# Low-weight products of features 128 to 191 on 64 rows of TensorE, two side by side into two PSUM banks

## The chip, the cores and the metric

The kernel runs on one core of one Trainium2 chip. The metric is the device time of one execution in microseconds (us); lower is better. A core has five engines with queues of their own: TensorE (PE, matrix products into PSUM; PEld is its weight load), VectorE (DVE), ScalarE (ACT), GpSimd (POOL) and SyncE (SP, which here only issues DMAs).

## What is computed

An attention-like step turns 8 x 3584 tokens of 192 features into 28672 rows, and a mixture of 8 experts with one expert for each token (top 1) follows.

```python
x_unf = x_pad[:, idx, :].reshape(B, S, K, H, group)          # K = 7 taps, H = 8 heads
out = np.einsum('bshk,bskhg->bshg', softmax(weight_gen), x_unf)
x = out.reshape(28672, 192)
e_idx = np.argmax(x @ w_gate, axis=1)
for e in range(8):
    h = np.maximum(x[mask] @ w1[e], 0.0)                     # 192 -> 1024
    ye = h @ w2[e]                                           # 1024 -> 192
    out[mask] = gate_w[mask, None] * eom[mask, e, None] * ye
```

## The kernel before

**Stages.** The tokens are worked through in 32 units of 896. For a unit, DVE and POOL multiply taps and weights and the sums are formed on PE or DVE; the rows are split into fp16 high and low parts, gated, and scattered by expert into a buffer in HBM (`srtd`). As soon as enough rows of an expert lie there, a *tile* of T rows (T = 256 or 384 in the first rounds, then 512, and at the end a mix of 512, 256 and 128) goes through the expert. There are 81 tiles. Until the last unit is scattered, tiles and attention run together; after that (the *late part*) only tiles are left.

**A tile.** `tile_load` (L944) issues on SP, in this order: `meta`, a transposing DMA of the rows into `xT`, and the expert's weights `wa` (L953, w1 in fp16 parts) and `wb` (w2). `xT` has three blocks of 128 partitions: block 0 is the high part of features 0 to 127, block 1 holds the high part of features 128 to 191 on partitions 0 to 63 and their low part on 64 to 127, block 2 is the low part of features 0 to 127.

**GEMM1** (`gemm1_unit`, L959). A *unit of GEMM1* fills one PSUM bank of 512 columns: nf = 512 // T blocks of 128 hidden features, five products each, all on 128 rows of the array:

```python
for q, (wo, k) in enumerate(((f * P, 0), (1024 + f * P, 0), (f * P, 2), (b3, 1), (b3 + 512, 1))):
    T_.matmul(ps[:, at + i * T : at + (i + 1) * T], lhsT=wa[:, wo : wo + P], rhs=xT[:, k, 0:T], start=(q == 0), stop=(q == 4), ...)
```

The fourth multiplies the high weights of features 128 to 191, which lie in `wa` twice (partitions 0 to 63 and 64 to 127), with block 1; the fifth multiplies their low weights, also stored twice, with block 1, so its lower half is low weight times low feature. `evac_steps` (L972) then empties the bank: ACT writes relu as fp16 (`hh`), DVE the rest (`hl`).

**GEMM2** (`gemm2_group`, L981) takes 128 rows of a tile: 24 products of 192 columns. `gemm_steps` (L1066) places two units of GEMM1, then a group of GEMM2, and so on. For T = 512 and 384 a tile has eight units (four twos), for 256 four, for 128 two.

**Order.** The program orders itself while it is built: each chain of steps yields the engine that it needs next, `Order.step` (L88) takes the chain that can start first by costs in the program (`tensor_cost`, L195, and others), and what comes out is the fixed order of each engine's queue. A change of a cost or of a step can so move any instruction.

**Weights.** `weight_steps` (L425) loads w1 and w2 of each expert, `split_steps` (L439) scales and splits them and stores them to HBM as `wd`, 3585 words of 4 bytes for each partition: 2048 for `wa`, 1537 for `wb`.

Of the kernel before, what the change touches and what calls it, by code (L numbers as in the profile page):

```python
# [9 lines left out]
F16 = mybir.dt.float16  # L10
BF16 = mybir.dt.bfloat16
F32 = mybir.dt.float32
I32 = mybir.dt.int32
# [3 lines left out]

P = 128
W = 194
WW = 3585  # L20
RMAX = 24
NE = 8
MASK = 0x3F800000
# [170 lines left out]

def tensor_cost(name, args, kwargs):  # L195
    o = kwargs.get("rhs", kwargs.get("in_"))
    return max(60, largest((o,), {}) + 6) * (4 if o.dtype == F32 else 1) / 2400.0


# [18 lines left out]
def kernel(ctx: ExitStack, tc: tile.TileContext, x, wg, wgate, wogate, w1, w2, cst, out):  # L218
    nc = tc.nc
    od = Order()  # L220
# [24 lines left out]
    late = []  # L245
# [89 lines left out]
    o = 256  # L335
# [89 lines left out]
    def weight_steps(stg):  # L425

        for e in range(NE):
            yield from take(st_free, SP)

            st1 = stg.tile([P, 1536], F32, tag="st1", name=f"st1_{e}")  # L430
            st2 = stg.tile([P, 1536], F32, tag="st2", name=f"st2_{e}")
            SP.dma_start(out=st1[:, 0:1024], in_=w1[e, 0:128, :])
            for h in range(2):
                SP.dma_start(out=st1[64 * h : 64 * h + 64, 1024:1536], in_=w1[e, 128:192, 512 * h : 512 * h + 512])
            SP.dma_start(out=st2.rearrange("p (c d) -> p c d", d=D), in_=w2[e].rearrange("(c p) d -> p c d", p=P))
            od.add(split_steps(e, st1, st2), (RANK_W, e), S)
            od.cur.t = od.now

    def split_steps(e, st1, st2):  # L439
        sqd = stg_sq.tile([P, 1536], BF16, tag="sqd", bufs=1, name=f"sqd{e}")  # L440
        ss = sp.tile([P, 2], F32, tag="wss", name=f"wss{e}")
        S.activation(sqd, st1, AF.Square, accum_out=ss[:, 0:1])
        yield S
        S.activation(sqd, st2, AF.Square, accum_out=ss[:, 1:2])
        yield from take(tr_free, T_)
        pg = ps[:, 1536:1538]
        T_.matmul(pg[:, 0:2], lhsT=ones32, rhs=ss, start=True, stop=True)
        yield V
        sc = sp.tile([P, 2], F32, tag="wsc", name=f"wsc{e}")
        inv = sp.tile([P, 2], F32, tag="winv", name=f"winv{e}")  # L450
        yield from scales(pg[:, 0:2], sc, inv, f"w{e}", tr_free)
        s1, s2 = sc[:, 0:1], sc[:, 1:2]
        yield from take(wa_free, S)
        wa = wp.tile([P, 1536], I32, tag="wa", bufs=WA, name=f"wpa{e}")
        wah = wa.bitcast(F16)

        for lo, n in ((0, 1024), (2048, 512)):
            src = st1[:, lo // 2 : lo // 2 + n]
            hi = wah[:, lo : lo + n]
            yield S  # L460
# [11 lines left out]
        wb = wp.tile([P, WW - 2048], I32, tag="wb", bufs=WB, name=f"wpb{e}")  # L472
# [9 lines left out]
        SP.dma_start(out=wd[e, :, 2048:WW], in_=wb)  # L482
        wb_free.append((od.cur.t, "wb"))
        state["weights"] += 1

# [458 lines left out]
    def tile_load(t, T, ti, i, writers, ka, kb):  # L944
# [6 lines left out]
        xT = gp.tile([P, 3, 512], F16, tag="xT", bufs=XB, name=f"xT{t}")  # L951
        loaded(SP.dma_start_transpose(out=xT[:, :, 0:T], in_=rows.bitcast(F16)[:, 0:384]), writers)
        wa = (late[0] if ka == "late" else wp).tile([P, 2048], I32, tag="wa", bufs=LATE_W if ka == "late" else WA, name=f"wa{t}")  # L953
        SP.dma_start(out=wa, in_=wd[bass.ds(e, 1), :, 0:2048].rearrange("a p c -> p (a c)"))
        wb = (late[0] if kb == "late" else wp).tile([P, WW - 2048], I32, tag="wb", bufs=LATE_W if kb == "late" else WB, name=f"wb{t}")
        SP.dma_start(out=wb, in_=wd[bass.ds(e, 1), :, 2048:WW].rearrange("a p c -> p (a c)"))
        return dict(t=t, T=T, G=Gn, units=8 // (512 // T), wa=wa.bitcast(F16), wb=wb.bitcast(F16), inv=wb.bitcast(F32)[:, 1536:1537], meta=meta, xT=xT, ka=ka, kb=kb, hh=[], hl=[], hl_t=0.0)

    def gemm1_unit(hp, d, u, at):  # L959

        t, T, wa, xT = d["t"], d["T"], d["wa"], d["xT"]
        nf = 512 // T
        hh = hp.tile([P, 512], F16, tag="hh", name=f"hh{t}_{u}")
        hl = hp.tile([P, 512], F16, tag="hl", name=f"hl{t}_{u}")
        for i in range(nf):
            f = u * nf + i
            b3 = 2048 + f // 4 * 1024 + f % 4 * P
            for q, (wo, k) in enumerate(((f * P, 0), (1024 + f * P, 0), (f * P, 2), (b3, 1), (b3 + 512, 1))):
                T_.matmul(ps[:, at + i * T : at + (i + 1) * T], lhsT=wa[:, wo : wo + P], rhs=xT[:, k, 0:T], start=(q == 0), stop=(q == 4), skip_group_check=True)
        od.add(evac_steps(d, ps[:, at : at + nf * T], hh[:, 0 : nf * T], hl[:, 0 : nf * T], at), (RANK_H,), S, T_.t + LAT_P)  # L970

    def evac_steps(d, src, hh, hl, at):  # L972
        S.activation(hh, src, AF.Relu)
# [7 lines left out]
    def gemm2_group(d, g, at):  # L981
# [4 lines left out]
        py = ps[:, at : at + D]  # L986
        nf = 512 // T
        for f in range(8):
            lo = (f % nf) * T + g * P
            hh = d["hh"][f // nf][:, lo : lo + P]  # L990
            hl = d["hl"][f // nf][:, lo : lo + P]
# [74 lines left out]
    def gemm_steps(hp):  # L1066
# [3 lines left out]
        while True:  # L1070
            moved = False
            if cur is None and ahead:
                cur, i = ahead.pop(0), 0
            if cur is not None and len(h_free) >= 2:
                for _ in range(2):
                    _, at = yield from take(hu_free, T_)
                    yield from take(h_free, T_)
                    od.cur.t = max(od.cur.t, cur["ready"])
                    gemm1_unit(hp, cur, i, at)
                    i += 1  # L1080
# [70 lines left out]
LAT_P = 0.3  # L1151
# [25 lines left out]
FIRST_G = ()  # L1177
DEFER = 6
WBX = 5.0
PAIRS = 0  # L1180
TURN_SP = True
GT = 1
# [22 lines left out]
```

## Time and profile before

| | |
|---|---|
| median of 3 runs | 1276.98 us (1276.81 to 1280.58) |
| the profiled execution | 1277.73 us, its span 1276.0 us |
| mean granted clock of TensorE | 0.977 |
| busy: PE, DVE, POOL, ACT | 1143.7, 997.5, 895.6, 602.5 us |
| moved by DMA | 300.24 MB |

The profile gives each engine's busy time, the idle time before a group of instructions and what ended it. A matmul's record begins when its columns start to enter and ends, by a model, when its result is out, so records of successive products overlap. A timeline row of n products lasts n - 1 pitches and one record; the pitch, start to start, is what a product costs in a full queue.

### The profile page before, as it was taken

To read this page: it belongs to the slowest core of one execution; us is meant where nothing else is said; L and a number is where in the kernel's file an instruction comes from. 1 tells how busy PE (TensorE), PEld (TensorE's weight loads), DVE (VectorE), ACT (ScalarE), POOL (GpSimd) and SP (SyncE) were. 2 spreads that over 40 slices of the span, in tenths; PEclk is the share of its full clock that TensorE was granted. 3 is DMA by queue.
4 is the path that set the end of the run, shared out by engine and by line. 5 is a ranking of instruction groups with operands and counts; after the bars stand their busy time and mean duration, and the time that the engine had idled before them with its cause. 6 is when DMAs were issued, how large, how long until landed. Compare 5 with 4: busy or idle time off the path is not lost.

```text
span 1276.0 us, 28173 instructions
## 1 busy us (share of the span) xinstructions
PE 1143.7 (90%) x9958; PEld 832.0 (65%) x9958; DVE 997.5 (78%) x2135; ACT 602.5 (47%) x1305; POOL 895.6 (70%) x773
## 2 busy tenths in 40 slices
PE   5788778888988898969999999999999999979998
PEld 2444347666655666646666666666667779868998
DVE  7899968888999898989999999989998633323332
ACT  3676444545544445534554545545455444433443
POOL 6769877878687689989688898798987544312222
PEclk9899988999999999989999999999999999999999
DMA  9887568888988677768886977876686789999993
GB/s 298 268 242 244 188 207 222 240 209 247 251 195 241 184 215 182 233 171 229 243 217 192 240 219 210 253 215 212 191 223 163 223 296 315 351 274 314 321 343 131
DMA packets 273054, 300.24 MB, mean 235 GB/s; under 512 B 211478, under 2 KB 232839, under 8 KB 262544
## 3 DMA queue, kind: packets, MB, share of 16 engines
q1 hardware_dynamic: 250928, 253.83, 69.0%
q0 software_dynamic: 21840, 44.30, 11.3%
q8 instruction: 78, 1.28, 0.4%
q14 instruction: 64, 0.52, 0.2%
q10 hardware_dynamic: 144, 0.31, 0.1%
HBM read 196.42 MB, written 62.01 MB: 203 GB/s over the span
## 4 chain that ended last, share of the span: by engine, by line
PE 38%; DVE 29%; DMA 11%; issue 9%; POOL 7%; SPq 4%; ACT 2%; POOLq 0%; DVEq 0%; ACTq 0%
PE ps L151 38%; DVE ps L151 12%; DVE hl L151 6%; SPq L125 4%; POOL gap L151 3%; DMA w<-in_wg_dram 2%; DMA wa<-wd 2%; DVE rt L151 2%; DVE vap L151 2%; DMA srtd<-rt,posi 2%; POOL srtd L151 2%; DMA wb<-wd 1%; POOL out_dram L151 1%; DVE cx L151 1%; DVE wpa L151 1%
## 5 line engine op out<-in xcount | busy, mean ns | idle before, releaser
L151 PE MATMUL ps<-xT,wa 128*128 128x512 f16 (+3 forms) x3240 | 556.5, 322 | 49.2 <-DMA wa<-wd 30.1
L151 PE MATMUL ps<-wb,hh 128*128 128x192 f16 x3696 | 479.3, 247 | 16.0 <-ACT ys L151 4.5
L151 PE MATMUL ps<-wb,hl 128*128 128x192 f16 x1848 | 456.2, 247 | 0.7 <-DVE hl L151 0.7
L151 DVE SCALAR_TENSOR_TENSOR hl<-ps,hh 128x512 f16<-128x512 f32 (+1 forms) x476 | 309.2, 665 | 182.2 <-ACT hh L151 181.8
L151 PEld LDWEIGHTS <-wa 128*128 128x128 f16 x3240 | 278.0, 99 | 238.9 <-issue 34.3
L151 POOL TENSOR_TENSOR gap<-x,w 128x960 f32<-128x960 f32 (+5 forms) x268 | 373.6, 1419 | 27.9 <-PE ps L151 15.3
L151 PEld LDWEIGHTS <-hh 128*128 128x128 f16 x3696 | 337.1, 98 | 63.7 <-issue 22.6
L151 ACT ACTIVATE hh<-ps 128x512 f16<-128x512 f32 (+1 forms) x476 | 274.4, 583 | 215.1 <-PE ps L151 211.5
L151 POOL DMA_INDIRECT out_dram<-ys,meta x216 | 214.2, 991 | 221.3 <-ACT ys L151 160.2
L151 POOL DMA_INDIRECT srtd<-rt,posi x224 | 231.3, 1033 | 92.1 <-issue 56.9
L151 ACT ACTIVATE ys<-ps,sc 128x192 f32<-128x192 f32 x231 | 97.1, 421 | 240.1 <-PE ps L151 152.0
L151 DVE TENSOR_TENSOR ps<-ps,gap 128x1344 f32<-128x1344 f32 x125 | 194.0, 1552 | 4.9 <-POOL gap L151 4.0
L151 PEld LDWEIGHTS <-hl 128*128 128x128 f16 x1848 | 181.6, 98 | 1.1 <-DVE hl L151 0.9
L151 PE MATMUL ps<-gap,cf 128*128 128x512 f32 x168 | 72.9, 574 | 0.2 <-POOL gap L151 0.2
L151 POOL TENSOR_TENSOR gap<-halo,w 128x1152 f32<-128x1152 f32 (+4 forms) x38 | 61.9, 1628 | 13.6 <-DVE w L151 7.4
L151 DVE SCALAR_TENSOR_TENSOR rt<-ps,sx,rt 128x448 f16<-128x448 f32 x64 | 57.8, 908 | 16.3 <-ACT rt L151 12.7
L151 PE MATMUL ps<-vap,cf 128*128 128x512 f32 (+1 forms) x126 | 57.8, 603 | 14.0 <-DVE vap L151 14.0
L151 PE MATMUL ps<-gm,gt 128*128 128x32 f16 x672 | 27.8, 177 | 36.3 <-ACT ys L151 10.0
L151 PEld LDWEIGHTS <-gt 128*128 128x128 f16 x672 | 25.1, 97 | 46.6 <-issue 38.4
L151 DVE TENSOR_TENSOR vap<-x,w 128x960 f32<-128x960 f32 (+4 forms) x31 | 54.7, 1789 | 0.0
L151 PEld LDWEIGHTS ps<-gap,cf 128*128 128x128 f32 x168 | 32.5, 203 | 31.6 <-issue 29.1
L151 ACT ACTIVATE rt<-ps 128x1344 bf16<-128x1344 f32 x32 | 41.3, 1291 | 18.5 <-DVE ps L151 9.5
(115 smaller groups left out, 813.8 us busy)
## 6 DMA issues: line engine op xcount, KB each, us to landing
wa<-wd SPq DMA_DIRECT2D x81, 1024.0 KB
wb<-wd SPq DMA_DIRECT2D x81, 768.5 KB
x<-in_x_dram SPq DMA_DIRECT2D x32, 672.0 KB
w<-in_wg_dram SPq DMA_DIRECT2D x32, 196.0 KB
wd<-wpb SPq DMA_DIRECT2D x8, 768.5 KB
st<-in_w_dram SPq DMA_DIRECT2D x8, 768.0 KB
st<-in_w_dram SPq DMA_DIRECT2D x8, 512.0 KB
wd<-wpa SPq DMA_DIRECT2D x8, 512.0 KB
```

The source lines that it names most:

```text
L125: r = f(*args, **kwargs)
L151: r = f(*args, **kwargs)
```

## The change

- GEMM1's fifth product, low weights of features 128 to 191, now takes 64 rows: low weights times the high part of the features alone (the product of low weight and low feature is no longer formed).
- `gemm1_pair` replaces `gemm1_unit`. It takes two banks and two units with blocks f = 2 f2 and 2 f2 + 1: four full products (of each block) into the first bank; then the 64-row products, for block 2 f2 on partitions 0 to 63 into the first bank and for block 2 f2 + 1 on partitions 64 to 127 into the second; then four full products into the second.
- For the lower 64 partitions `xT` gets a fourth block: `again_steps` copies, on ACT, once for each tile, the high part of features 128 to 191 from partitions 0 to 63 to partitions 64 to 127.
- The low weights are stored once: `wa` goes from 2048 to 1792 words for each partition (1024 to 896 KB for a tile), `wd` from 3585 to 3329. The stores of `wpa` become six for each expert instead of five, and two loads of w1 are read in pieces of 128 columns.
- The cost of a product with 64 rows becomes half of its columns and 0.05 us.

```diff
-WW = 3585
+WA_W = 1792
+WW = 3329
...
+    if o.shape[0] == 64:
+        return 0.5 * largest((o,), {}) / 2400.0 + SWITCH
...
-                SP.dma_start(out=st1[64 * h : 64 * h + 64, 1024:1536], in_=w1[e, 128:192, 512 * h : 512 * h + 512])
+                SP.dma_start(
+                    out=st1[64 * h : 64 * h + 64, 1024:1536].rearrange("p (c d) -> p c d", d=P),
+                    in_=w1[e, 128:192, :].rearrange("p (c two d) -> p two c d", two=2, d=P)[:, h])
...
-                SP.dma_start(out=wd[e, 64 * q : 64 * q + 64, 1024 + 512 * h : 1536 + 512 * h], in_=wa[64 * h : 64 * h + 64, 1024:1536])
+                SP.dma_start(out=wd[e, 64 * q : 64 * q + 64, 1024 + 256 * h : 1280 + 256 * h], in_=wa[64 * h : 64 * h + 64, 1024:1280])
+        SP.dma_start(out=wd[e, :, 1536:1792], in_=wa[:, 1280:1536])
...
+    def again_steps(d):
+        S.copy(d["xT"][64:128, 3, 0 : d["T"]], d["xT"][0:64, 1, 0 : d["T"]])
+        d["again"] = True
...
-    def gemm1_unit(hp, d, u, at):
+    def gemm1_pair(hp, d, u):
+        for v in range(2):
+            _, at = yield from take(hu_free, T_)
+            yield from take(h_free, T_)
+            if u + v == 0:
+                yield T_, lambda: "again" in d
...
+            if v == 1:
+                for i in range(nf):
+                    for s in range(2):
+                        lo, f2, to = 64 * s, u // 2 * nf + i, ats[s] + i * T
+                        T_.matmul(ps[:, to : to + T], lhsT=wa[lo : lo + 64, 3072 + f2 * P : 3072 + f2 * P + P], rhs=xT[lo : lo + 64, 1 + 2 * s, 0:T], start=(s == 1 and i == 0), stop=(s == 0), skip_group_check=True)
+                od.add(evac, (RANK_H,), S, T_.t + LAT_P)
+            for i in range(nf):
...
+                for q, (wo, k) in enumerate(((f * P, 0), (1024 + f * P, 0), (f * P, 2), (b3, 1))):
+                    T_.matmul(ps[:, at + i * T : at + (i + 1) * T], lhsT=wa[:, wo : wo + P], rhs=xT[:, k, 0:T], start=(v == 0 and q == 0 and i == 0), stop=(v == 1 and q == 3), skip_group_check=True)
+            evac = evac_steps(d, ps[:, at : at + nf * T], hh[:, 0 : nf * T], hl[:, 0 : nf * T], at)
+        od.add(evac, (RANK_H,), S, T_.t + LAT_P)
...
                 cur, i = ahead.pop(0), 0
+                od.add(again_steps(cur), (RANK_H,), S, max(od.now, cur["ready"]))
...
+SWITCH = 0.05
```

Where the order moves, two places. On SP, where the first tile is loaded (`x8` and `w8` are the inputs of attention unit 8, `wpb7` is the store of the last expert's w2, `meta0`, `xT0`, `wa0`, `wb0` are tile 0), the queue had before:

```order
L125 DMA w8_1158<-in_wg_dram 128x392
L125 DMA halo_83<-in_x_dram 112x1152
L125 DMA halo_83<-in_x_dram 15x1152
L125 DMA x8_1162<-in_x_dram 128x1344
L125 DMA wd_79<-wpb7_1120 128x1537
L125 TENSOR_LOAD ti2_0_1146
L125 ISA x2
L125 TENSOR_LOAD ti2_0_1146
L125 ISA x3
L125 DMA meta0_1331<-srtd_78 128x2x2
```

The inputs of unit 8 stood ahead of the last store of weights and of tile 0. In the changed kernel the same queue has:

```order
L126 ISA x3
L126 DMA meta0_1275<-srtd_78 128x2x2
L126 ISA
L126 DMA_TRANSPOSE xT0_1277<-srtd_78 128x3x256
L126 ISA
L126 DMA wa0_1279<-wd_79 128x1792
L126 ISA
L126 DMA wb0_1281<-wd_79 128x1537
L126 DMA w8_1327<-in_wg_dram 128x392
L126 DMA halo_83<-in_x_dram 112x1152
L126 DMA halo_83<-in_x_dram 15x1152
L126 DMA x8_1331<-in_x_dram 128x1344
```

Tile 0 now stands one attention unit earlier, ahead of the inputs of unit 8, and its `wa` is smaller. On ACT, in the middle of the program, where tile 21 or 22 is emptied (`hh22_4` is unit 4 of tile 22, `ys21` a group of GEMM2 of tile 21), the queue had before:

```order
L151 ACTIVATE hh22_4_7733<-ps_82 128x512
L151 ACTIVATE hh22_5_7746<-ps_82 128x512
L151 ACTIVATE ys21_7493<-ps_82,sc21_7494 128x192
L151 ACTIVATE hh22_6_7789<-ps_82 128x512
L151 ACTIVATE hh22_7_7800<-ps_82 128x512
L151 ACTIVATE hh23_0_7839<-ps_82 128x512
```

The two units of each two followed each other, with nothing of the next tile between. In the changed kernel, at tile 21:

```order
L152 ACTIVATE hh21_4_7409<-ps_82 128x512
L152 ACTIVATE hh21_5_7416<-ps_82 128x512
L152 ACTIVATE ys20_7308<-ps_82,sc20_7309 128x192
L152 ACTIVATE hh21_6_7461<-ps_82 128x512
L152 COPY xT22_7258<-xT22_7258 64x512
L152 ACTIVATE hh21_7_7472<-ps_82 128x512
```

The copy for the next tile, 22, stands between the last two bank emptyings of tile 21, and it waits for the landing of `xT22`.

## Rows read from the trace of the kernel before

**Rows 1.** The page, part 2: the span in 40 equal slices of 31.9 us, busy share of each engine in tenths, the granted clock and the DMA engines.

```profile
PE   5788778888988898969999999999999999979998
DVE  7899968888999898989999999989998633323332
POOL 6769877878687689989688898798987544312222
PEclk9899988999999999989999999999999999999999
DMA  9887568888988677768886977876686789999993
```

**Rows 2.** Busy time by stage; the columns are the stretch, its length, then PE, PEld, DVE, ACT and POOL with their instructions, the granted clock, the DMA share and GB/s.

```profile
0.00:200.00 200.00, 152.11 (x674) 83.01 (x675) 170.10 (x323) 106.89 (x185) 153.58 (x111) 0.93 0.75 234
200.00:400.00 200.00, 169.87 (x1516) 125.78 (x1514) 186.30 (x411) 95.78 (x234) 153.40 (x134) 0.97 0.86 232
400.00:1000.00 600.00, 557.54 (x4807) 393.26 (x4805) 546.91 (x1218) 292.28 (x661) 502.55 (x442) 0.99 0.76 213
1000.00:1100.00 100.00, 100.00 (x1009) 81.30 (x1007) 43.13 (x114) 41.63 (x87) 41.48 (x43) 1.00 0.93 298
1100.00:1150.00 50.00, 43.39 (x509) 38.18 (x507) 13.74 (x20) 16.32 (x34) 13.29 (x14) 0.97 0.96 304
1150.00:1276.00 126.00, 120.78 (x1454) 110.46 (x1452) 37.36 (x54) 49.57 (x107) 31.27 (x32) 1.00 0.88 275
```

**Rows 3.** The same stretches, of the instructions on the tile `wa` alone (GEMM1): the columns are PE and PEld, the clock, the DMA share and GB/s of the whole core.

```profile
0.00:200.00 200.00, 10.82 (x74) 8.63 (x75) 0.93 0.75 234
200.00:400.00 200.00, 96.01 (x479) 46.28 (x476) 0.97 0.86 232
400.00:1000.00 600.00, 305.46 (x1283) 121.56 (x1284) 0.99 0.76 213
1000.00:1100.00 100.00, 56.40 (x433) 33.83 (x431) 1.00 0.93 298
1100.00:1150.00 50.00, 24.16 (x269) 18.00 (x267) 0.97 0.96 304
1150.00:1276.00 126.00, 63.63 (x710) 49.64 (x708) 1.00 0.88 275
```

**Rows 4.** Groups of PE's instructions with their shapes: count, busy us, mean ns of one record, idle time before.

```profile
L151 PE MATMUL ps<-xT,wa 128*128 128x512 f16 x1680 | 400.6, 382 | 32.7 <-DMA wa<-wd 16.9 <-DVE hl L151 14.9
...
L151 PE MATMUL ps<-xT,wa 128*128 128x128 f16 x880 | 52.7, 219 | 3.1 <-DMA wa<-wd 3.1
L151 PE MATMUL ps<-xT,wa 128*128 128x384 f16 x280 | 51.9, 332 | 9.2 <-DMA wa<-wd 5.9 <-DVE hl L151 3.4
L151 PE MATMUL ps<-xT,wa 128*128 128x256 f16 x400 | 51.4, 289 | 4.2 <-DMA wa<-wd 4.2
```

**Rows 5.** Timeline of PE, one row of products for each size of tile: start, duration, count.

```profile
423.15 2.32 PE L151 MATMUL ps<-xT,wa 128*128 128x512 f16 x10
...
235.09 1.79 PE L151 MATMUL ps<-xT,wa 128*128 128x384 f16 x10
...
1224.98 2.35 PE L151 MATMUL ps<-xT,wa 128*128 128x256 f16 x20
...
1220.77 2.40 PE L151 MATMUL ps<-xT,wa 128*128 128x128 f16 x40
```

**Rows 6.** Timeline of PE where the form of the products changes: 32 columns after 192, with a weight load for each; then in attention from 32 columns to transposes to fp32.

```profile
427.21 0.25 PE L151 MATMUL ps<-wb,hl 128*128 128x192 f16 x1
427.29 0.46 PE L151 MATMUL ps<-gm,gt 128*128 128x32 f16 x12
...
169.97 0.30 PE L151 MATMUL ps<-gm,gt 128*128 128x32 f16 x6
170.12 0.33 PE L151 MATMUL ps<-ident,rt 128*128 128x128 f16 x3
170.29 2.47 PE L151 MATMUL ps<-vap,cf 128*128 128x512 f32 x6
```

**Rows 7.** PE's waits, longest in total first: us, times, longest.

```profile
PE ps L151 <- DMA wa<-wd: 30.1, 11, 9.6
PE ps L151 <- DVE hl L151: 19.0, 23, 3.8
PE ps L151 <- ACT ys L151: 17.1, 29, 2.2
```

**Rows 8.** SP's queue about the first tile's load (start, duration), and the DMA issues of the weights of a tile.

```profile
148.44 0.35 SPq L125 DMA_DIRECT2D w<-in_wg_dram  x1
...
164.11 0.41 SPq L125 DMA_DIRECT2D meta<-srtd  x1
...
170.64 0.34 SPq L125 DMA_DIRECT2D w<-in_wg_dram  x1
...
wa<-wd SPq DMA_DIRECT2D x81, 1024.0 KB
wb<-wd SPq DMA_DIRECT2D x81, 768.5 KB
```

**Rows 9.** ACT's copies of fp16 and its bank emptying, with shapes: count, busy us, mean ns.

```profile
L151 ACT ACTIVATE hh<-ps 128x512 f16<-128x512 f32 x420 | 247.1, 595 | 195.2 <-PE ps L151 191.9 <-issue 3.1
...
L151 ACT COPY gt<-ps 128x768 f16<-128x768 f16 x18 | 14.3, 794 | 18.5 <-PE ps L151 18.3
...
L151 ACT COPY gt<-ps 128x384 f16<-128x384 f16 x6 | 2.9, 479 | 4.2 <-PE ps L151 4.2
```

More of the change, by code (lines that the diff above doesn't have):

```diff
@@ L471, in split_steps @@
         yield from take(wb_free, S)
-        wb = wp.tile([P, WW - 2048], I32, tag="wb", bufs=WB, name=f"wpb{e}")
+        wb = wp.tile([P, WW - WA_W], I32, tag="wb", bufs=WB, name=f"wpb{e}")
         wbh = wb.bitcast(F16)
@@ L481, in split_steps @@
         yield SP
-        SP.dma_start(out=wd[e, :, 2048:WW], in_=wb)
+        SP.dma_start(out=wd[e, :, WA_W:WW], in_=wb)
         wb_free.append((od.cur.t, "wb"))
@@ L950, in tile_load @@
         loaded(SP.dma_start(out=meta[:, 0:Gn, :], in_=rows[:, W - 2 : W].rearrange("(g p) c -> p g c", p=P)), writers)
[L951 to L954, printed above, removed]
@@ L955, in tile_load @@
-        wb = (late[0] if kb == "late" else wp).tile([P, WW - 2048], I32, tag="wb", bufs=LATE_W if kb == "late" else WB, name=f"wb{t}")
-        SP.dma_start(out=wb, in_=wd[bass.ds(e, 1), :, 2048:WW].rearrange("a p c -> p (a c)"))
-        return dict(t=t, T=T, G=Gn, units=8 // (512 // T), wa=wa.bitcast(F16), wb=wb.bitcast(F16), inv=wb.bitcast(F32)[:, 1536:1537], meta=meta, xT=xT, ka=ka, kb=kb, hh=[], hl=[], hl_t=0.0)
-    def gemm1_unit(hp, d, u, at):
-        t, T, wa, xT = d["t"], d["T"], d["wa"], d["xT"]
[L962 to L970, printed above, removed]
+        xT = gp.tile([P, 4, 512], F16, tag="xT", bufs=XB, name=f"xT{t}")
@@ new lines, in tile_load @@
+        loaded(SP.dma_start_transpose(out=xT[:, 0:3, 0:T], in_=rows.bitcast(F16)[:, 0:384]), writers)
+        wa = (late[0] if ka == "late" else wp).tile([P, WA_W], I32, tag="wa", bufs=LATE_W if ka == "late" else WA, name=f"wa{t}")
+        SP.dma_start(out=wa, in_=wd[bass.ds(e, 1), :, 0:WA_W].rearrange("a p c -> p (a c)"))
+        wb = (late[0] if kb == "late" else wp).tile([P, WW - WA_W], I32, tag="wb", bufs=LATE_W if kb == "late" else WB, name=f"wb{t}")
+        SP.dma_start(out=wb, in_=wd[bass.ds(e, 1), :, WA_W:WW].rearrange("a p c -> p (a c)"))
@@ new lines, in tile_load @@
+        return dict(t=t, T=T, G=Gn, units=8 // (512 // T), wa=wa.bitcast(F16), wb=wb.bitcast(F16), inv=wb.bitcast(F32)[:, 1536:1537], meta=meta, xT=xT, ka=ka, kb=kb, hh=[], hl=[], hl_t=0.0)
+    def again_steps(d):
+        S.copy(d["xT"][64:128, 3, 0 : d["T"]], d["xT"][0:64, 1, 0 : d["T"]])
+        d["again"] = True
+        return
+        yield
+    def gemm1_pair(hp, d, u):
+        t, T, wa, xT = d["t"], d["T"], d["wa"], d["xT"]
+        nf, ats = 512 // T, []
+        for v in range(2):
[3 more added lines that the diff above has]
+                yield T_, lambda: "again" in d
+            od.cur.t = max(od.cur.t, d["ready"])
+            ats.append(at)
+            hh, hl = [hp.tile([P, 512], F16, tag=tag, name=f"{tag}{t}_{u + v}") for tag in ("hh", "hl")]
+            if v == 1:
[5 more added lines that the diff above has]
+            for i in range(nf):
+                f2 = u // 2 * nf + i
+                f = 2 * f2 + v
+                b3 = 2048 + v * 512 + f2 * P
+                for q, (wo, k) in enumerate(((f * P, 0), (1024 + f * P, 0), (f * P, 2), (b3, 1))):
+                    T_.matmul(ps[:, at + i * T : at + (i + 1) * T], lhsT=wa[:, wo : wo + P], rhs=xT[:, k, 0:T], start=(v == 0 and q == 0 and i == 0), stop=(v == 1 and q == 3), skip_group_check=True)
+            evac = evac_steps(d, ps[:, at : at + nf * T], hh[:, 0 : nf * T], hl[:, 0 : nf * T], at)
+        od.add(evac, (RANK_H,), S, T_.t + LAT_P)
@@ L988, in gemm2_group @@
         for f in range(8):
-            lo = (f % nf) * T + g * P
-            hh = d["hh"][f // nf][:, lo : lo + P]
-            hl = d["hl"][f // nf][:, lo : lo + P]
+            lo = f % (2 * nf) // 2 * T + g * P
+            v = f // (2 * nf) * 2 + f % 2
+            hh = d["hh"][v][:, lo : lo + P]
+            hl = d["hl"][v][:, lo : lo + P]
             w2h = wb[:, f * D : (f + 1) * D]
@@ L1073, in gemm_steps @@
                 cur, i = ahead.pop(0), 0
+                od.add(again_steps(cur), (RANK_H,), S, max(od.now, cur["ready"]))
             if cur is not None and len(h_free) >= 2:
[L1075 to L1080, printed above, removed]
+                yield from gemm1_pair(hp, cur, i)
+                i += 2
                 moved = True
```

## The prediction

> **What bounds the kernel now.** I read the slices first, then the busy time by stage, then PE's own waits. The slices [rows 1] show PE at 9 almost throughout from a third of the span on, while DVE and POOL fall to 3 and 2 in the last quarter. By stage [rows 2], PE is busy for 557.5 of the 600 us from 400 to 1000, beside DVE at 546.9 and POOL at 502.5; between 1000 and 1100 it is busy all the time with DVE at 43. So the late part is PE's alone, the middle is PE's with DVE close behind, and only before 400 us has PE room (152 of 200, then 170 of 200). The clock granted is near full in all of it, so durations need no correction. What PE waits for [rows 7] is led by weights, `wa`, with 30.1 us in 11 waits; the DMA engines are at 0.88 to 0.96 in the late part [rows 2]. A matmul here costs its pitch, not its record: 10 products of 512 columns take 2.32 us [rows 5] and one record 382 ns [rows 4], so a pitch is (2.32 - 0.38) / 9 = 0.216 us.
>
> **What is removed from PE.** In the same way the pitch is (1.79 - 0.332) / 9 = 0.162 us at 384 columns, (2.35 - 0.289) / 19 = 0.108 at 256 and (2.40 - 0.219) / 39 = 0.056 at 128 [rows 4, 5]. A tile has 40 products of GEMM1, so there are 1680 / 40 = 42 tiles of 512, 7 of 384, 10 of 256 and 22 of 128 [rows 4]. I count in *pairs of units*: four for a tile of 512 or 384, two for 256, one for 128, that is 168, 28, 20 and 22, in all 238. If the two 64-row streams run at the same time, a pair of units gives back one pitch at 512 and 384, two at 256 and four at 128: 168 x 0.216 + 28 x 0.162 + 20 x 0.216 + 22 x 0.224 = 36.3 + 4.5 + 4.3 + 4.9 = 50 us of PE.
>
> **What is added on PE.** The trace has no product on fewer than 128 rows, so the price of going into that form of the array and out again is bounded by other rows. First, the second product starts behind the first: products of 32 columns, each with its own weight load, follow each other at (0.46 - 0.18) / 11 = 0.026 us [rows 6], so I take 0.026 for each pair of units. Then the change of form, twice for each pair. The low end is zero, or below it by nothing, since a product can't start before its queue reaches it: going from 192 to 32 columns, from products to transposes and from fp16 to fp32 costs no more than the pitch of the earlier ones; six products of 32 columns at 169.97 are followed by transposes at 170.12, 0.025 us for each [rows 6]. The high end is a full emptying of the array, the part of a record that outlasts its pitch, 382 - 216 = 166 ns. I take a third of it, 55 ns, an estimate: these rows of changed form, the nearest, stand at zero, but none of them splits the rows of the array, over which sums must not be in flight when it is split. [...]
>
> So a pair of units pays 0.026 + 2 x 0.055 = 0.136 us and keeps 0.216 - 0.136 = 0.080 (0.026 at 384). Where: of 3240 products of GEMM1, 433 + 269 + 710 = 1412 stand after 1000 us [rows 3]; less all of size 128 (880) and seven tiles of size 256 (280) 252 are left, 6.3 tiles of 512, so 22 + 14 + 25 = 61 pairs of units, worth 61 x 0.08 = 4.9 us in full, as nothing else is late there. From 400 to 1000 there are 1283 / 10 = 128 of them, 10.2 us, of which I count 0.9, PE's busy share: 9.2. The other 49 (28 of them at 384) lie before 400 us, where PE has idle time: 28 x 0.026 + 21 x 0.08 = 2.4, half counted, 1.2. Together 15 us.
>
> One rule speaks against the change. The Trainium skill, TensorEngine Tiling (Array Packing), section Tiling Modes, says that changing the tiling mode, unlike changing the tile within it, drains TensorE; it names no price, and no run here shows it. By the low end of my bounds the sum above would be 37 us instead of 15; by a drain for the whole 166 ns it would turn to a loss, a rival below.
>
> **Bytes.** `wa` falls by 128 of 1024 KB, with `wb` 768.5 KB unchanged [rows 8]: 81 x 128 KB = 10.6 MB less. An eighth of the 30.1 us of waits for `wa` [rows 7] is 3.8 us. The bounds are 0 and some 10 us, as in the late part PE's waits stand behind full DMA engines.
>
> **Order.** Tile 0 moves on SP ahead of the inputs of unit 8, so one attention unit earlier; these loads are issued at 148.4 and 170.6 us for two successive units and tile 0 at 164.1 [rows 8]. A unit is 22 us, PE is idle for 24% of the first 200 us [rows 2], so at most some 5 us of later PE work fits in earlier; I take 3. Below zero is possible too, as the units' own work waits behind the tile, down to -3.
>
> **Copies on ACT.** From 794 ns at 768 columns and 479 at 384 [rows 9] a copy is 0.16 + T x 0.00082: 0.58 us at 512, 0.27 at 128; 42 x 0.58 + 7 x 0.48 + 10 x 0.37 + 22 x 0.27 = 37 us in all. ACT is busy for 292 of 600 us in the middle [rows 2], and PE has four full products, 0.86 us, to do before it meets the copy's result, so this cover hides a copy at 512 columns if ACT is free. The copy is queued ahead of the last bank of the earlier tile and waits for `xT`; behind it stand that bank's `hh`, DVE's `hl`, and later GEMM2. As `xT` is issued ahead of `wa` on the same queue, PE would mostly wait for `wa` anyhow. I charge 2 us for all of it, with bounds 0 and 81 x 0.2 = 16, a third of one emptying of 595 ns [rows 9] each time. Without the cover the copies would cost their 37 us.
>
> The eight added stores and the smaller pieces of the weight loads (8 issues of about 0.6 us, on a queue with idle stretches such as 150 to 164 us [rows 8]) I take as 1 us. DVE's and POOL's instructions keep number and size.
>
> **Sum.** -15 - 3.8 - 3 + 2 + 1 = -19 us. The profiled execution took 1277.7 us, 0.7 over the median of the runs; from the median, 1277 - 19 = 1258 us, with 1247 to 1268 as its own range.
>
> **The rivals.**
>
> *Nothing is paid for the change of form.* Then a pair of units pays 0.026 alone and keeps 0.19: 61 x 0.19 + 128 x 0.19 x 0.9 + (28 x 0.136 + 21 x 0.19) / 2 = 11.6 + 21.9 + 3.9 = 37 us, with the other terms -41: 1236. For it speaks every row of changed form [rows 6]; against it, that none of these splits the array. The Trainium skill, TensorE: Matmul & The Clock Gate, Part 3, reports four products on 32 rows each running together 3.07 times as fast; that bears on the side by side, not on the change, and no run here shows it.
>
> *Each change of form empties the array.* Price 0.166 twice, so 0.026 + 0.332 = 0.358 for each pair of units against 0.216 saved, a loss of 0.142 (0.196 at 384). Place: between the fourth full product and the first of 64 rows, and again behind the second. 61 x 0.142 + 128 x 0.142 x 0.95 + 0.7 x (28 x 0.196 + 21 x 0.142) = 8.7 + 17.3 + 5.9 = 32 us, and with the other terms -4: about 1305, slower. It decides from (0.216 - 0.026) / 2 = 95 ns for each change on. The rule of the Trainium skill quoted above would be this case if the drain is a full one.
>
> *The two streams don't run side by side.* Then the second costs its pitch as before, nothing is saved on PE, and only bytes and order remain: about 1273, and worse by what the change of form costs.
>
> *DVE becomes the bound in the middle.* It is busy for 546.9 of 600 us [rows 2], and the second bank must be free one product earlier, while waits for `hl` are already 19 us [rows 7]. Then the 9.2 us of the middle vanish: about 1268.
>
> **How the numbers follow.** The forecast has 0.36; the free change 0.18; the emptying 0.26; one after the other 0.12 (of it 0.03 faster, 0.07 within 0.3%, 0.02 slower); DVE 0.08. 0.3%, about what a measurement of this kernel can tell from no change, is 4 us. Faster is 0.36 + 0.18 + 0.03 + 0.08 = 0.65, same 0.07, slower 0.28. The range must reach most of both outer cases: 1234 to 1304.
>
> **What would show it.** Right: the record of the 64-row product in the second bank starts about 0.03 us behind the first, and from the fourth full product's start to the next full one's is 0.216 + 0.216 + 0.136 = 0.57 us at 512 columns. At 0.46 the change is free, at 0.79 it empties the array, and at 0.65 or more with the second starting a whole pitch behind they don't run together. Waits for `wa` should fall to about 26 us. I am wrong if PE's waits for DVE or for ACT's copy grow by more than 10 us, or if the late part does not shorten although pairs of units do.

## The result, and the profile after

The changed kernel takes 1290.48 us (median of 9 runs, 1284.81 to 1298.48) beside 1279.81 us for the kernel before (9 runs, 1276.52 to 1283.93): a ratio of 1.0089, 95% interval [1.0062, 1.0116]. It is slower by some 11 us, where 19 us less were forecast. The profiled execution took 1289.56 us, its span is 1287.8 us.

The page of the changed kernel, part 2, the same rows as [rows 1], in slices of 32.2 us:

```profile
PE   5783989988778999999959999999899999999998
...
DVE  8897949888989899999978999989989553333232
POOL 6676696938969788788989687888887544422222
PEclk9996999989789999999979999999999999999999
DMA  9878387887857868878659967869658688989995
```

In the fourth slice (97 to 129 us) PE is at 3 tenths and its granted clock at 6, where the kernel before had 8 and 9. Busy time by stage, to be laid beside [rows 2]:

```profile
0.00:200.00 200.00, 145.12 (x657) 77.65 (x658) 156.09 (x322) 106.66 (x188) 144.00 (x108) 0.91 0.76 235
200.00:400.00 200.00, 168.81 (x1432) 113.41 (x1430) 179.30 (x404) 99.39 (x234) 148.76 (x128) 0.92 0.75 201
400.00:1000.00 600.00, 559.90 (x4794) 373.40 (x4792) 552.02 (x1205) 313.96 (x691) 504.67 (x443) 0.98 0.76 208
1000.00:1100.00 100.00, 99.92 (x948) 72.30 (x946) 44.86 (x128) 44.80 (x94) 45.77 (x47) 1.00 0.78 244
1100.00:1150.00 50.00, 48.16 (x554) 39.92 (x552) 16.44 (x24) 22.49 (x51) 16.64 (x17) 1.00 0.92 292
1150.00:1288.00 138.00, 127.18 (x1588) 111.35 (x1586) 38.72 (x56) 57.86 (x130) 32.26 (x33) 0.98 0.90 274
```

Both kernels have the same number of products, so the counts tell how far the work has come. By 400 us the changed kernel has started 657 + 1432 = 2089 of them, the kernel before 674 + 1516 = 2190 [rows 2]. It is 101 behind there and 114 behind at 1000 us. (Products differ in size; by PE's busy time it is 313.9 us beside 322.0 at 400 us.) At some 0.1 us for each product from 400 us on (876 us for the other 7800 or so [rows 2]) that is the 11.8 us by which the span grew. So in this execution the time was lost before 400 us, where PE has room, and the stage that was to give the gain, PE's own work, gave nothing back.

**The products themselves.** PE's timeline of the changed kernel: one row for each size of tile, to be laid beside [rows 5]; then the pair of units at 1052.13 again in overlapping narrow windows, so that a row holds two or three products.

```profile
1052.13 2.32 PE L152 MATMUL ps<-xT,wa 128*128 128x512 f16 x10
...
1052.78 0.70 PE L152 MATMUL ps<-xT,wa 128*128 128x512 f16 x3
...
1053.09 0.71 PE L152 MATMUL ps<-xT,wa 64*128 64x512 f16 x3
...
1053.41 0.60 PE L152 MATMUL ps<-xT,wa 128*128 128x512 f16 x2
...
266.69 1.84 PE L152 MATMUL ps<-xT,wa 128*128 128x384 f16 x10
...
1203.58 2.34 PE L152 MATMUL ps<-xT,wa 128*128 128x256 f16 x20
...
1224.28 2.38 PE L152 MATMUL ps<-xT,wa 128*128 128x128 f16 x40
```

Ten products of a pair of units take 2.32 us, exactly as before [rows 5]; at 384 columns 1.84 where it was 1.79, at 256 and 128 0.01 and 0.02 less. The narrow rows show why. The fourth full product starts at 1052.78 and the 64-row products at 1053.09, 0.31 us later, where the pitch is 0.216. Three products that begin at 1052.78 are done in 0.70, which is 0.31 and one record of 0.39: the second 64-row product starts with the first (the starts are 4 ns apart). So they do run side by side. The next full product starts at 1053.41, 0.32 us behind, and the one after it 0.60 - 0.38 = 0.22 us later (225 ns by the starts). Between the fourth full product and the second one behind the change lie 312 + 4 + 319 + 225 = 860 ns, where four pitches were 4 x 216 = 864. A pair of units gives back 4 ns.

The Trainium skill, TensorE: Matmul & The Clock Gate, Part 3, has products on different rows of the array start within about 4 ns of each other: the trace agrees, with 4 ns. The Trainium skill, TensorEngine Tiling (Array Packing), section Tiling Modes, has every change of the tiling mode drain TensorE and gives no price: the trace agrees that it costs, 96 ns on the way in and 103 on the way out at 512 columns. That the array is drained in this time, the trace does not show.

**Pairs that do not share.** The second 64-row product opens the second bank, and where DVE has not yet emptied that bank, PE waits between the two products. One such place (the row begins with the second 64-row product, the four full ones behind it are merged into it), and the 64-row products of two widths with the idle time before them:

```profile
260.87 1.87 PE L152 MATMUL ps<-xT,wa 64*128 64x384 f16 x5 [3.23 <-DVE hl L152]
...
L152 PE MATMUL ps<-xT,wa 64*128 64x512 f16 x336 | 73.0, 389 | 9.2 <-DVE hl L152 7.8 <-ACT xT L152 1.1
L152 PE MATMUL ps<-xT,wa 64*128 64x384 f16 x56 | 12.2, 337 | 5.7 <-DVE hl L152 5.2 <-ACT xT L152 0.3
```

By the starts in the trace, the second product comes 27 ns to 3.6 us behind the first in 36 of the 238 pairs of units, and in 30 of them more than a pitch behind. In these 30 the two do not run side by side, and both changes of form are paid all the same. With 1.3 us at 256 columns, 14.3 of the 18.9 us that PE waits for `hl` fall between the two.

**Where the 0.1 us go.** The weight loads of the same pair of units in the changed kernel (the bracket is the idle time before the load):

```profile
1052.05 0.61 PEld L152 LDWEIGHTS <-wa 128*128 128x128 f16 x4
1053.09 0.10 PEld L152 LDWEIGHTS <-wa 64*128 64x128 f16 x2 [0.42 <-issue]
1053.41 0.55 PEld L152 LDWEIGHTS <-wa 128*128 128x128 f16 x4 [0.23 <-issue]
```

In a run of full products a load goes ahead beside the product before it: the four loads are over 0.61 us after the first began, while their products start over 0.65 us and from 0.08 us later on. By that the load for the first 64-row product could start at 1052.78, with the fourth full product; it starts at 1053.09, with its own product. On the way back it is the same at 1053.41. Load and product of the new form come together, and no load is done in advance over a change; by the starts in the trace it is so in every stretch between full products of 512 columns, in and out, where the load starts 4 to 5 ns ahead of its product.

**Waits of PE** (us in total, times, longest), beside [rows 7]:

```profile
PE ps L152 <- DMA wa<-wd: 26.1, 9, 7.0
PE ps L152 <- DVE vap L152: 20.6, 2, 13.7
PE ps L152 <- DVE hl L152: 18.9, 18, 3.2
PE ps L152 <- ACT ys L152: 14.2, 24, 2.1
```

Waits for `wa` fell by 4.0 us, with `wa` at 896 KB (DMA issues, beside [rows 8]):

```profile
wa<-wd SPq DMA_DIRECT2D x81, 896.0 KB
```

ACT's copies at 512 columns, by form: count, busy us, mean ns, and what it waited for before them.

```profile
L152 ACT COPY xT<-xT 64x512 f16<-64x512 f16 x42 | 25.9, 617 | 3.9 <-DMA xT<-srtd 2.9
```

617 ns, where 580 were reckoned; with the smaller ones the copies come to 40 us in all instead of 37.

**What the new order did.** SP's queue in the changed kernel (start, duration), where tile 0 is loaded, beside [rows 8], and where the loads of a later tile stand:

```profile
140.79 0.35 SPq L126 DMA_DIRECT2D w<-in_wg_dram  x1
...
163.12 0.41 SPq L126 DMA_DIRECT2D meta<-srtd  x1
...
169.24 0.34 SPq L126 DMA_DIRECT2D w<-in_wg_dram  x1
...
343.07 0.37 SPq L126 DMA_DIRECT2D x<-in_x_dram  x1
358.31 9.62 SPq L126 DMA_TRANSPOSE gt<-rt  x7
369.63 0.42 SPq L126 DMA_DIRECT2D meta<-srtd  x1
370.20 1.48 SPq L126 DMA_TRANSPOSE xT<-srtd  x1
371.88 0.42 SPq L126 DMA_DIRECT2D wa<-wd  x1
```

Tile 0 stands one attention unit earlier in the queue, but its `meta` is issued only 1.0 us earlier, 163.12 for 164.11. Further on, seven transposing DMAs of attention stand ahead of the loads of a tile, so `wa` is issued at 371.88, and between 349 and 400 us PE waits 7.0 us for it, in one piece:

```profile
PE ps L152 <- DMA wa<-wd: 7.0, 1, 7.0
```

The kernel before has the same kind of stall, but at other places. A reading of one trace can't tell whether it is these stalls that make the loss; the experiments ask for the order as a whole.

### The profile page after: what moved, and what is told of

The parts are those of the page before. It is cut to its first block, busy times and chain, and to the rows that moved or that the text cites. A ratio compares the mean times of both kernels' runs of the same rounds, so it can differ in the third digit from the quotient of the medians.

```text
span 1287.8 us, 28254 instructions
## 1 busy us (share of the span) xinstructions
PE 1149.1 (89%) x9958; PEld 788.0 (61%) x9958; DVE 987.4 (77%) x2135; ACT 645.2 (50%) x1386; POOL 892.1 (69%) x773
## 4 chain that ended last, share of the span: by engine, by line
PE 43%; DVE 19%; DMA 11%; POOL 10%; issue 9%; SPq 5%; ACT 3%; POOLq 0%; DVEq 0%; ACTq 0%
PE ps L152 43%; DVE ps L152 7%; POOL gap L152 5%; DMA wa<-wd 5%; SPq L126 5%; POOL srtd L152 3%; DVE hl L152 3%; DVE vap L152 3%; DMA srtd<-rt,posi 2%; DVE rt L152 2%; POOL out_dram L152 2%; DMA w<-in_wg_dram 1%; DVE cx L152 1%; ACT rt L152 1%; DMA gt<-rt 1%
## 5 line engine op out<-in xcount | busy, mean ns | idle before, releaser
L152 PE MATMUL ps<-xT,wa 128*128 128x512 f16 (+7 forms) x3240 | 559.8, 323 | 47.4 <-DMA wa<-wd 26.1
L152 PEld LDWEIGHTS <-wa 128*128 128x128 f16 (+1 forms) x3240 | 230.1, 97 | 287.5 <-issue 160.1
L152 POOL DMA_INDIRECT srtd<-rt,posi x224 | 229.3, 1024 | 87.8 <-issue 57.6
L152 DVE TENSOR_TENSOR vap<-x,w 128x960 f32<-128x960 f32 (+4 forms) x31 | 58.5, 1911 | 1.7 <-PE ps L152 1.6
L152 PEld LDWEIGHTS ps<-vap,cf 128*128 128x128 f32 x126 | 24.2, 202 | 44.9 <-issue 22.9
```

Source lines behind the costliest of these rows:

```text
L152: r = f(*args, **kwargs)
```

## The experiments

"Before" is always the kernel before, timed in the same runs. The last column is the ratio to it.

| kernel | median, us | before, us | ratio [95%] |
|---|---|---|---|
| e1_full_rows | 1287.36 | 1278.03 | 1.0071 [1.0050, 1.0093] |
| e2_old_new_costs | 1287.75 | 1278.03 | 1.0076 [1.0048, 1.0105] |
| e3_cost_as_measured | 1304.02 | 1278.03 | 1.0199 [1.0168, 1.0230] |
| e4_no_copy | 1304.69 | 1278.03 | 1.0187 [1.0156, 1.0219] |
| e5_old_order | 1349.63 | 1351.41 | 0.9990 [0.9972, 1.0008] |
| e6_old_order_full | 1346.99 | 1351.41 | 0.9973 [0.9950, 0.9996] |
| e7_apart | 1388.08 | 1351.41 | 1.0292 [1.0256, 1.0328] |
| e8_old_order_again | 1274.72 | 1278.32 | 0.9973 [0.9954, 0.9993] |
| e9_old_order_full_again | 1271.59 | 1278.32 | 0.9954 [0.9935, 0.9974] |
| e10_changed_again | 1287.91 | 1278.32 | 1.0084 [1.0057, 1.0111] |
| e11_old_booked_dearer | 1289.64 | 1279.62 | 1.0084 [1.0067, 1.0101] |
| e12_old_booked_cheaper | 1291.10 | 1279.62 | 1.0084 [1.0067, 1.0101] |

**Is it the 64-row form?** The changed kernel, in its own order, with the two low-weight products on 128 rows:

```diff
-        S.copy(d["xT"][64:128, 3, 0 : d["T"]], d["xT"][0:64, 1, 0 : d["T"]])
+        S.copy(d["xT"][:, 3, 0 : d["T"]], d["xT"][:, 1, 0 : d["T"]])
...
-                        T_.matmul(ps[:, to : to + T], lhsT=wa[lo : lo + 64, 3072 + f2 * P : 3072 + f2 * P + P], rhs=xT[lo : lo + 64, 1 + 2 * s, 0:T], start=(s == 1 and i == 0), stop=(s == 0), skip_group_check=True)
+                        T_.matmul(ps[:, to : to + T], lhsT=wa[:, 3072 + f2 * P : 3072 + f2 * P + P], rhs=xT[:, 1 + 2 * s, 0:T], start=(s == 1 and i == 0), stop=(s == 0), skip_group_check=True)
```

> The changed kernel with its order, copies and bytes, but its 64-row products made 128-row ones, with all 128 partitions of the low weights and of the copied block (the sums so get products that do not belong in them). No change of form is left. Price theory (each change of form costs PE about 0.1 us, as much as the shared stream saves, so the form is neutral, and the rest of the change makes the loss): within 4 us of the changed kernel, 1287 to 1296. Form theory (the 64-row form costs more than its starts show, through the clock or stalls behind it): 8 us or more faster than the changed kernel.

1.0071, within the interval of the changed kernel's 1.0089: with the new form taken out most of the loss stays. The weight loads of a pair of units in this kernel run through without a gap:

```profile
1053.04 1.91 PEld L153 LDWEIGHTS <-wa 128*128 128x128 f16 x10
```

So the form costs about what it saves, and something else makes the loss.

**Is it the order alone?** The kernel before, instruction for instruction, with the new booked cost for its fifth product:

```diff
+    if HALF:
+        return 0.5 * largest((o,), {}) / 2400.0 + 0.05
...
+                globals()["HALF"] = q == 4
                 T_.matmul(ps[:, at + i * T : at + (i + 1) * T], lhsT=wa[:, wo : wo + P], rhs=xT[:, k, 0:T], start=(q == 0), stop=(q == 4), skip_group_check=True)
+        globals()["HALF"] = False
```

> The kernel before, all instructions as they were, with only the cost that the program books for the fifth product cut to that of a 64-row one, so that it orders itself anew. Order theory (the loss comes from another order of the same work): off the kernel before by 4 to 15 us, rather slower. Coupling theory (the loss comes from the pair's second bank and the copy on ACT, which this kernel does not have): within 4 us of the kernel before.

1.0076: the same instructions in another order lose nearly all that the changed kernel loses. Their loss lies at another place. PE's waits from 1040 us to the end in this kernel:

```profile
PE ps L152 <- DMA wa<-wd: 12.2, 5, 5.6
```

and in the kernel before:

```profile
PE ps L151 <- DMA wa<-wd: 6.6, 3, 3.5
```

**Would the right cost mend it?** The booked cost of a 64-row product as the trace has it:

```diff
-SWITCH = 0.05
+SWITCH = 0.103
```

> The changed kernel with the booked addition for a 64-row product at 0.103 us in place of 0.05, about what the trace shows, so the same work in another order. Order theory: off the changed kernel by 4 us or more, rather faster, 1272 to 1288. Coupling theory: within 4 us of it.

1.0199, a miss in sign: the truer cost gives the worse order. PE's waits for `wa` in this kernel:

```profile
PE ps L152 <- DMA wa<-wd: 40.8, 9, 7.7
```

**Is it the coupling over ACT?** No copies and no wait for them; both 64-row products read block 1:

```diff
-            if u + v == 0:
-                yield T_, lambda: "again" in d
...
-                        T_.matmul(ps[:, to : to + T], lhsT=wa[lo : lo + 64, 3072 + f2 * P : 3072 + f2 * P + P], rhs=xT[lo : lo + 64, 1 + 2 * s, 0:T], start=(s == 1 and i == 0), stop=(s == 0), skip_group_check=True)
+                        T_.matmul(ps[:, to : to + T], lhsT=wa[lo : lo + 64, 3072 + f2 * P : 3072 + f2 * P + P], rhs=xT[lo : lo + 64, 1, 0:T], start=(s == 1 and i == 0), stop=(s == 0), skip_group_check=True)
...
-                od.add(again_steps(cur), (RANK_H,), S, max(od.now, cur["ready"]))
```

> The changed kernel without the copies on ACT and the waits for them; the second product of two reads the low features that lie on its partitions in place of the high ones, so half of the low-weight products are others. Coupling theory: 6 us or more faster than the changed kernel, 1284 or less. Order theory: off by a few us either way, as its order moves too; PE waits for the copies only 2.2 us in the trace of the changed kernel, so 0 to 3 us faster of itself.

1.0187: not faster but slower, by more than the few us that the order theory gave. The order moved once more, and the waits for `wa` are 58.3 us. For the copies alone this run decides nothing, because the order went with them. That they would explain the loss finds no support.

**The change in the order of before.** To hold the order, the program books what the kernel before booked (a full fifth product at its old place, the old sizes of the DMAs) and neither the copies nor the added stores; the units are placed one by one as before. Beside it the same with fifth products of 128 rows, and with 64-row products that share no stretch (each unit changes the form on its own, 476 stretches instead of 238):

```diff
+    def book(self, **kwargs):
+        c, own = self.order.cur, self.cost("", (), kwargs)
+        self.t = max(self.t, c.t + self.before) + own
+        c.t = max(c.t, self.t + self.after)
...
-    if o.shape[0] == 64:
-        return 0.5 * largest((o,), {}) / 2400.0 + SWITCH
...
-        SP.dma_start(out=wd[e, :, 1536:1792], in_=wa[:, 1280:1536])
+        nc.sync.dma_start(out=wd[e, :, 1536:1792], in_=wa[:, 1280:1536])
...
+            T_.book(rhs=xT[:, 0, 0:T])
...
-                od.add(again_steps(cur), (RANK_H,), S, max(od.now, cur["ready"]))
+                nc.scalar.copy(cur["xT"][64:128, 3, 0 : cur["T"]], cur["xT"][0:64, 1, 0 : cur["T"]])
```

> The change (64-row products of two units side by side, copies, smaller weights) in the order of the kernel before: costs are booked as there, the copies and the added stores are issued without being booked, and of PE's queue only the place of 12 products differs. Price theory (two changes of form at 0.1 us eat what a pair of units saves, and the order makes the loss): 1272 to 1281, the kernel before less 2 us of PE and up to 4 of waits for weights. Coupling theory (copies on ACT and the second bank): slower than the kernel before by 6 us or more, since these are all still there.

> As the run in the old order, but the fifth product of each unit stands where it stood and takes 128 rows (the sums so get products that do not belong in them); no change of form, and copies on ACT over 128 partitions. Bytes and copies alone: 1271 to 1280, within 3 us of the run in the old order by the price theory, 10 or more slower than it if the shared stream is worth its 50 us less a small price.

> As the run in the old order, but each unit's 64-row products stand at the end of their unit, so no two units share a stretch: 476 stretches in place of 238 and each stream for itself. Price theory (0.1 us for each change of form): 238 x (0.216 + 0.2) = 97 us of PE more than the run in the old order, 1355 to 1375. If the 0.2 us were a price of two streams starting together and not of the form: about 48 us more or less, 1320 to 1330.

These three were timed in a set of runs in which the kernel before itself took 1351 us, so the times expected were missed. Why it took so long is not shown: e11_old_booked_dearer and e12_old_booked_cheaper ran on the chip of the same number, and there it took 1279.62 us. PE waited 52.4 us for `ys` in e5_old_order, but 17.7 us in e8_old_order_again, which is the same kernel in another set. So the three are read against one another and against the kernel before of their own set alone.

How far the order is held can be read from the traces, by the names of the tiles that a product writes and reads. Of the 9958 products in PE's queue none stands at another place than in the kernel before in e6_old_order_full, e7_apart and e9_old_order_full_again, and 33 do in e5_old_order and e8_old_order_again; 3724 do in the changed kernel, 3073 in e2_old_new_costs. The changed kernel and e1_full_rows agree in all.

In the order of before the loss is gone (0.9990 and 0.9973). Twice the stretches cost 1388.08 - 1349.63 = 38 us, less than the 97 expected, and PE's busy time grew by 69.6 us. By the time alone the other theory, with some 48 us, would be nearer. The starts decide between the two: at 512 columns a stretch of one stream takes 312 + 319 + 226 = 857 ns from the full product before it to the second one behind it, where three pitches are 648. That is 209 ns for the two changes, as with two streams. PE's waits for `ys` fell from 52.4 to 35.5 us, so a part of the price went where PE had waited. The page, part 1, with the streams shared and then apart:

```profile
PE 1176.1 (87%) x9958; PEld 799.7 (59%) x9958; DVE 999.4 (74%) x2135; ACT 638.9 (47%) x1386; POOL 896.4 (66%) x773
```

```profile
PE 1245.7 (90%) x9958; PEld 800.3 (58%) x9958; DVE 1001.0 (72%) x2135; ACT 642.3 (46%) x1386; POOL 896.0 (65%) x773
```

The price of a change of form is real; sharing a stretch between two streams pays it back and no more.

The two kernels in the order of before and the changed kernel, timed in another set, with the kernel before at 1278.32 us:

> The change in the order of the kernel before, once more, beside the changed kernel on the same chip; in the first run of it the kernel before took 1351 us, with PE waiting 52 us for ys, so PE was less of a bound. Price theory: within 0.4% of the kernel before on either side, and at least 0.5% faster than the changed kernel. Coupling theory: with the changed kernel, 0.6% or more slower than the kernel before.

> 128-row products, smaller weights and copies in the order of the kernel before, once more. Price theory: within 0.4% of the run with 64 rows in the same order; bytes and copies are worth 0 to 0.4% against the kernel before.

> The changed kernel itself, as the control on this chip: 0.6 to 1.2% slower than the kernel before, whichever theory holds.

The same change gives 0.9973 in the order of before and 1.0084 in its own: 13.2 us lie between the two, with the same products, copies and bytes. With 128-row products the kernel is 3.1 us faster still (0.9954), and with such products too the two orders lie apart: 0.9954 here and 1.0071 in e1_full_rows.

**Is it this order, or any other?** Again the kernel before, instruction for instruction, with the booked cost of its fifth product a little up and a little down (shown is the first; the second has -0.02 for 0.05):

```diff
-    return max(60, largest((o,), {}) + 6) * (4 if o.dtype == F32 else 1) / 2400.0
+    return max(60, largest((o,), {}) + 6) * (4 if o.dtype == F32 else 1) / 2400.0 + (0.05 if HALF else 0.0)
```

> The kernel before, instruction for instruction, with only the booked cost of the fifth product of GEMM1 raised by 0.05 us (it was lowered in the run of the kernel before with the new costs, which lost 0.76%). If the costs of the kernel before are a setting around which any other order is worse, this loses too, 0.5 to 2%. If the direction counts, that is if a fifth product booked too cheap lets the units come too early and one booked dearer gives the loads more room, it is within 0.3% or faster, 1268 to 1281 us.

> The kernel before, instruction for instruction, with only the booked cost of the fifth product lowered by 0.02 us, a fifth to a third of the step taken by the new costs. If any other order is worse, it loses 0.5 to 2% like the large step. If the loss grows with the error in the booked cost, it loses 0.1 to 0.3%, which is within what can be told from no change, some 1280 us.

Both lose, 10.0 and 11.5 us by the medians. Up by 0.05 or down by 0.02 us: of these two steps neither the size nor the sign showed in the time, only that the order is another one. The places differ too. Products in each stretch of the span, from the busy time of PE in each kernel (windows of 0 to 400, 400 to 1000 and 1000 to the end; a product over an edge counts on both sides):

| kernel | to 400 us | 400 to 1000 | from 1000 |
|---|---|---|---|
| before | 2187 | 4807 | 2969 |
| changed | 2086 | 4794 | 3084 |
| e10_changed_again | 2131 | 4805 | 3027 |
| e1_full_rows | 2080 | 4791 | 3089 |
| e2_old_new_costs | 2188 | 4795 | 2981 |
| e11_old_booked_dearer | 2183 | 4742 | 3037 |
| e12_old_booked_cheaper | 2179 | 4702 | 3083 |
| e8_old_order_again | 2158 | 4801 | 3005 |
| e9_old_order_full_again | 2182 | 4817 | 2964 |

The changed kernel is behind by 400 us, the kernel before with a cost moved a little in the middle (65 and 105 products), the one with the new costs hardly at all until 1000 us and then in the late part. The changed kernel and e10_changed_again are one program, and their counts at 400 us differ by 45, so differences of that size tell little. There is no one stall that all of them share.

But a stall can be told to go with an order. PE's waits for `wa` between 295 and 400 us, in the kernel before and in the changed one:

```profile
PE ps L151 <- DMA wa<-wd: 1.5, 1, 1.5
...
PE ps L152 <- DMA wa<-wd: 11.5, 2, 7.0
```

In e10_changed_again and e1_full_rows, which have the order of the changed kernel, they are 14.0 and 12.6 us, in e8_old_order_again and e9_old_order_full_again, which have that of before, 1.8 and 1.5. So this stall belongs to the order and not to the 64-row form. It is not the whole account: between 500 and 600 us PE waits 9.6, 9.4 and 9.9 us for `wa` in the three kernels in the order of before, and not at all in the other three. What makes one order faster in the sum is not shown.

## Why the prediction was wrong

**The side by side** was right where the second bank is free: there both streams run at once, and 4 ns were measured where 26 were charged. But the sum took it for all 238 pairs of units, and in 36 of them PE waits for that bank between the two products.

**The price of a change of form** failed. I took "a third of it, 55 ns", between zero and the emptying of 166 ns; it is 96 ns in and 103 + 9 out. A pair of units pays 212 ns and gives back 216, so the 80 ns that it was to keep are 4. At 384 columns a pair of units is 0.05 us longer instead of 0.026 shorter. The third was a choice that no run shows. The term of -15 us is so about 0 by the pitches: 168 x -4 + 28 x 50 + 20 x -7 + 22 x -10 ns = +0.4 us. The kernels with 64 and with 128 rows in one order differ by 3.1 us in favour of 128 rows; the pitches don't show these 3 us. A likely place are the pairs that do not share: they pay the changes, some 0.21 us, and get back no common pitch, by the starts an estimate of 30 x 0.21 = 6 us of PE. PE's busy time is longer by that order, 1149.1 us beside 1140.0 in e1_full_rows, and a part of it goes into shorter waits for `hl`, 18.9 us beside 22.6. No run tries it alone. The reason for the low guess was that all rows of changed form stood at zero [rows 6], and they do; but none of them splits the rows of the array, as the prediction said itself, and so they were no neighbours of this case. The rival that empties the array put the point of decision at 95 ns for each change, (216 - 26) / 2. With 4 ns between the streams in place of 26 it is 106, and the two changes came to 104 on average: so by its form the change decides nothing.

**The order** failed in sign, and this made the result. The term was -3 us, with some 5 to be won at most and 3 to be lost, and it weighed one place, tile 0. There it was wrong as well: the loads came 1.0 us earlier and not a unit. But the other instructions moved too, since every booked cost shapes the queues of all engines. Measured by the pair of kernels that differ in the order, this term is +13.2 us (1287.91 - 1274.72), and kernels that hold nothing of the change but a moved cost lose 9.7 to 11.5 us by the medians. All the other orders that were tried lose, by 0.8 to 2%. So the order of the kernel before is better than these; what makes it so stays open, and whether there is a still better one was not tried. No bound in the prediction covered such a loss.

**Bytes, copies and stores** were forecast at -3.8 + 2 + 1 = -0.8 us and come to 1271.59 - 1278.32 = -6.7 us together, by the kernel with 128-row products in the order of before, interval about -8.3 to -3.3. They were not parted. Waits for `wa` fell from 30.1 [rows 7] to 21.9 us in that kernel.

**The sum** now reads -6.7 for bytes, copies and stores, +3.1 for the 64-row form, +13.2 for the order: +9.6 us, which is 1287.91 - 1278.32 of the same runs, as it must be, since each is a difference of two of its medians. Each term has an uncertainty of some 2 to 3 us.

**The signs to watch.** 0.57 us from the fourth full product to the next full one were forecast and 0.635 measured, beside the three pitches of 0.648 that they replace; the waits for `wa`, "about 26", are 26.1, but that tells nothing here, since orders with less of them (23.1 us with the new costs in the kernel before) lose as well, and e1_full_rows, with the same bytes in the same order, has 30.0. Of the ways to be wrong that the prediction named, a wait of PE for the copies is not seen, 2.2 us in all, and its waits for DVE grew by 7.5 us, from 72.2 to 79.7, less than the 10 named.

The change itself, in the order of before, is a little faster than both kernels: 1274.72 us, 0.9973 [0.9954, 0.9993] of the time before. By the sum above this gain is that of bytes, copies and stores, and the 64-row form takes a part of it away. With fifth products of 128 rows it would be 0.9954, but that kernel forms other sums, so this is a bound and no version to use.

## What to carry to other kernels

Where a program orders itself by booked costs, time a new cost on the old instructions first: here that alone was worth +0.8%, more than anything else that the change did. Where a part of the work changes to fewer rows of the array, count the stretches: each has to save more than some 0.21 us, one product of 512 columns, and so several products of that form should stand in a row, which no run here tried. Two streams that are to share a stretch need both of their banks free at its start. A price for which the trace has no near row should be carried through the sum at both ends, and where the point of decision lies between them the forecast is open.

## What the runs showed that was not expected

- Going from 128 to 64 rows and back costs about as much at every width: 96 and 103 ns at 512 columns, 96 and 103 at 384 (258 and 265 ns at a pitch of 162), and by the starts in the trace 96 and some 93 at 256 and 128. It is no emptying of 166 ns, and also nothing that a weight load done ahead hides: the load of the new form starts with its product.
- A stretch costs the same with one stream as with two. In the kernel with the streams apart, at 256 columns, eight full products, two of 64 rows, and eight full ones again:

```profile
1150.81 1.04 PE L157 MATMUL ps<-xT,wa 128*128 128x256 f16 x8
1151.78 0.39 PE L972 MATMUL ps<-xT,wa 64*128 64x256 f16 x2
1152.10 1.05 PE L157 MATMUL ps<-xT,wa 128*128 128x256 f16 x8
1153.08 0.39 PE L972 MATMUL ps<-xT,wa 64*128 64x256 f16 x2
```

  Eight full products start over 1150.81 to 1151.78, 0.97 us, where eight pitches of 0.109 are 0.87: 0.10 us on the way in. From 1151.78 to 1152.10 there are 0.32 us for two pitches of 0.109: 0.10 on the way out.
- The granted clock was lower in the new order, 0.92 for 0.97 between 200 and 400 us [rows 2]. By slices it fell where PE had stood idle: 6 in the one in which PE was at 3 tenths (97 to 129 us), 7 and 8 in those from 322 to 386 us, where PE was at 7 and waited 7.0 us for `wa`. A slice mixes the clock's two levels, 1.2 and 2.4 GHz. In the changed kernel's trace 96 us stand at the lower one, 59 us in that of the kernel before, but PE was busy in only 52 and 49 us of them. A product of 512 columns takes 427 ns there for 216, so these 3 us more cost some 1.5 us, an estimate: the lower clock goes with the stalls and explains little of the 11 us.
